# Expert weight forms kept in DRAM by the first token half and read back by the second, in a three-stage float32 kernel

## The chip, the core and the metric

One core of one Trainium2 chip runs the whole program. The metric is the device time of one execution in microseconds; the kernel before has a median of 1330.94 us in three runs (1329.68 to 1335.48).

## What is computed

The reference runs a retention layer, a dense gated layer and a mixture of eight experts with a soft gate on 1536 tokens (2 sequences of 768), model width 512.

```python
state = gamma * state + outer(k[t], v[t]); y[t] = scale * q[t] @ state     # 8 heads of 64
h = x @ w_in; x = (h * clip(h + 3, 0, 6) / 6) @ w_out                      # 2048 hidden
P = exp(x @ w_gate - max)                                                 # then 8 times: rows, columns normalised
for e in range(8):
    out += P[:, e:e + 1] * (relu(x @ w1[e]) @ w2[e])                      # 1024 hidden each
```

## The kernel before

**High and low parts.** Every float32 operand of the dense layer and the experts is split in two: a high part, which ScalarE rounds to TensorE's fast float32 format (`fp32r`), and a low part, the rest, which VectorE gets by subtracting (helper `parts`, lines 499 to 501). A product is three matmuls: high x high, high x low, low x high.

**Stages.** Up to about 60 us: retention. Then the dense layer (lines 348 and 375) to 322.6 us. Then the experts, to the end. Tokens go through the experts in two halves of 768 (`NU` = 2). The 8 experts' 64 hidden tiles of 128 are taken two at a time: 32 pairs per half (`NPR`), 64 in all (`NIT`), each half with the same weights. 

**A pair.** `pair(i)` (line 599) computes the hidden tiles of pair i with a Strassen-like scheme: seven products of sums of weight blocks with sums of token blocks (`product`, line 585, tile `h`, 42 matmuls with 384 columns) in place of eight. ScalarE copies a bank out (line 604, tiles `p`, `u`), VectorE adds another bank to it (line 603), and ScalarE and VectorE make ReLU's high and low parts (`gh`, `gl`, lines 595 and 596). A TensorE product that goes on in a bank waits until the copy of it is out. `outputs(n)` (line 638) multiplies the hidden tiles of two pairs by the second weight (line 660, tile `acc`, 512 columns) and VectorE adds them to `o`, scaled by the gate (line 673). Iteration `it` of the main loop (line 800) weaves pairs 2it and 2it+1 with the outputs of the two pairs before, one chunk of three matmuls at a time, so that 42 + 36 matmuls stand in a pair; the first two pairs have no outputs to weave in.

**Weight forms.** For each pair `w1_forms` (line 503) reads a raw tile of 128 x 2 x 512 (`raw`, DMA of 512 KB, line 494) and makes seven forms of 128 x 256, high and low: four ScalarE and eight VectorE instructions. `w2_parts` (line 528) does the second weight: two and two. Both are generators of `jobs`, one step after each product of the pair: in pair i the first-weight forms of pair i+1, then the second-weight parts of pair i. Each raw tile's successor (two pairs later) is loaded when its forms have read it. The first-weight forms have two buffers, the second-weight parts four. The second half makes the same forms again from the same raw weights.

**The start of the experts.** The forms of pairs 0 and 1 are made while the dense layer ends; the first two raw tiles of the second weight are loaded when the dense layer's memory is free (pool `m2`). In pair 0, the parts of the second weight begin after the fifth product (`slot > 4`).

**The turn.** Before pair 32 the token forms of the second half are made (`x_forms`, nine steps, high and low parts `xh`, `xl`). To cover this, eight chunks of outputs run ahead (`ALONE`), and the rest of `x_forms` and then the forms of pair 33 follow in pair 32. The first half's output tiles (`out`, 256 KB each) are stored in that iteration.

**Order.** The program is issued in the order in which it is written; each engine takes its own instructions in that order. All DMAs here are issued by SP on one queue, and an SP instruction that waits holds back all behind it.

Of the kernel before, what the change touches and what calls it, by code (L numbers as in the profile page):

```python
# [10 lines left out]
F32R = mybir.dt.float32r  # L11
# [9 lines left out]
P = 128  # L21
# [6 lines left out]
BLK = 512  # L28
# [9 lines left out]
NPR = E * F2T // 2  # L38
NIT = NU * NPR
# [17 lines left out]
def kernel(  # L57
# [11 lines left out]
    nc = tc.nc  # L69
    f32 = lambda t: t.bitcast(F32)  # L70
# [6 lines left out]
    def pool(name, side, **kw):  # L77
        open_[name] = c = ExitStack()
        ctx.callback(c.close)
        return c.enter_context(tc.tile_pool(name=name, side=side, **kw))  # L80

    const = pool("const", "left", bufs=1)
    sk = pool("sk", "left", bufs=2)
    xo = pool("xo", "left", bufs=NU)
    xa = pool("xa", "left", bufs=NBLK - 1)
# [20 lines left out]
    raw_t, w_t, pools = {}, {}, {}  # L106
# [379 lines left out]
    B11, T2, T1, T3, B21, B22, T4 = range(7)  # L486
    xf, w1_t, w2_t, raw1, raw2, q_t = {}, {}, {}, {}, {}, {}

    def load_pair(i, part):
        if i >= NIT:  # L490
            return
        f = 2 * (i % NPR)
        t = pools["m2" if part else "m"].tile([P, 2, BLK], F32, tag=f"raw{part}", name=f"raw{part}", bufs=2)
        nc.sync.dma_start(
            out=t, in_=we_in[f:f + 2, :, part * BLK:(part + 1) * BLK].rearrange("t p c -> p t c")
        )
        (raw1, raw2)[part][i] = t

    def parts(hi, lo, t):
        nc.scalar.activation(out=hi, in_=t, func=AF.Copy)  # L500
        nc.vector.tensor_tensor(out=lo, in0=t, in1=f32(hi), op=ALU.subtract)  # L501

    def w1_forms(i):

        r = raw1.pop(i)
        H2 = BLK // 2
        hi = pools["m"].tile([P, 7, H2], F32R, tag="w1hi", name="w1hi", bufs=2)
        lo = pools["m"].tile([P, 7, H2], F32R, tag="w1lo", name="w1lo", bufs=2)
        a11, a12, a21, a22 = (r[:, f, k * H2:(k + 1) * H2] for f in range(2) for k in range(2))
        t = pools["m"].tile([P, 4, H2], F32, tag="s", name="s", bufs=2)  # L510
        parts(hi[:, A11:A12 + 1], lo[:, A11:A12 + 1], r[:, 0].rearrange("p (k c) -> p k c", k=2))
        yield True
        nc.vector.tensor_tensor(out=t[:, S1 - S1], in0=a21, in1=a22, op=ALU.add)
        yield True
        nc.vector.tensor_tensor(out=t[:, S3 - S1], in0=a11, in1=a21, op=ALU.subtract)
        yield True
        nc.vector.tensor_tensor(out=t[:, S2 - S1], in0=t[:, S1 - S1], in1=a11, op=ALU.subtract)
        parts(hi[:, A22], lo[:, A22], a22)
        yield True
        nc.vector.tensor_tensor(out=t[:, S4 - S1], in0=a12, in1=t[:, S2 - S1], op=ALU.subtract)  # L520
        load_pair(i + 2, 0)
        yield True
        for n in range(2):
            parts(hi[:, S1 + 2 * n:S3 + 1 + 2 * n], lo[:, S1 + 2 * n:S3 + 1 + 2 * n], t[:, 2 * n:2 * n + 2])
            yield True
        w1_t[i] = (hi, lo)

    def w2_parts(i):
        r = raw2.pop(i)
        hi = pools["m2"].tile([P, 2, BLK], F32R, tag="w2hi", name="w2hi", bufs=4)  # L530
        lo = pools["m2"].tile([P, 2, BLK], F32R, tag="w2lo", name="w2lo", bufs=4)
        for f in range(2):
            parts(hi[:, f], lo[:, f], r[:, f])
            yield True
        load_pair(i + 2, 1)
        w2_t[i] = (hi, lo)

    def x_forms(u):

        b11, b21, b12, b22 = (  # L540
            y2[u][:, 2 * k:2 * k + 2, j * SB:(j + 1) * SB] for j in range(2) for k in range(2)
        )
        xf.clear()

        def form(n, t):
            xf[n] = tuple(pools["xf"].tile([P, 2, SB], F32R, tag=f"x{n}{p}", name=f"x{p}") for p in "hl")
            parts(*xf[n], t)

        def tmp():
            t = pools["m"].tile([P, 4, BLK // 2], F32, tag="s", name="s", bufs=2)  # L550
            return t.rearrange("p a b -> p (a b)")[:, 0:2 * SB].rearrange("p (k c) -> p k c", k=2)

        form(B11, b11)
        yield True
        form(B21, b21)
        yield True
        t1 = tmp()
        nc.vector.tensor_tensor(out=t1, in0=b12, in1=b11, op=ALU.subtract)
        t2 = tmp()
        nc.vector.tensor_tensor(out=t2, in0=b22, in1=t1, op=ALU.subtract)  # L560
        yield True
        form(T2, t2)
        yield True
        form(T1, t1)
        yield True
        t4 = tmp()
        nc.vector.tensor_tensor(out=t4, in0=b21, in1=t2, op=ALU.subtract)
        t3 = tmp()
        nc.vector.tensor_tensor(out=t3, in0=b22, in1=b12, op=ALU.subtract)
        yield True  # L570
        form(T3, t3)
        yield True
        form(B22, b22)
        yield True
        form(T4, t4)
        yield True
# [22 lines left out]
    def pair(i):  # L599

        tmp = lambda n: pools["m2"].tile([P, SB], F32, tag=n, name=n, bufs=2)
        bank = lambda n: ps_s.tile([P, BLK], F32, tag=n, name="h")
        add = lambda out, a, b: nc.vector.tensor_tensor(out=out, in0=a, in1=b, op=ALU.add)  # L603
        copy = lambda out, a: nc.scalar.activation(out=out, in_=a, func=AF.Copy)  # L604

        bx = bank("s0")
        product(i, bx, A11, B11, True, True)
        p1 = tmp("p1")
        copy(p1, bx[:, 0:SB])
        yield  # L610
        by = bank("s1")
        product(i, by, A12, B21, True, True)
        yield
        add(p1, by[:, 0:SB], p1)
        product(i, bx, S2, T2, False, True)
        u2 = tmp("u2")
        copy(u2, bx[:, 0:SB])
        yield
        relu_parts(i, 0, 0, p1)
        bz = bank("r")  # L620
        product(i, bz, S1, T1, True, True)
        p5 = tmp("p5")
        copy(p5, bz[:, 0:SB])
        yield
        product(i, bx, S3, T3, False, True)
        add(p5, bx[:, 0:SB], p5)
        yield
        product(i, bz, S4, B22, False, True)
        relu_parts(i, 1, 1, p5)
        yield  # L630
        add(u2, bz[:, 0:SB], u2)
        product(i, bx, A22, T4, False, True)
        yield
        relu_parts(i, 0, 1, u2)
        relu_parts(i, 1, 0, bx[:, 0:SB])
        yield
# [44 lines left out]
    def drain(it):  # L681
        for _ in it:
            pass
# [7 lines left out]
    with tc.manual_schedule():  # L691
# [59 lines left out]
        forming = None  # L751
# [3 lines left out]
        for s in range(NSF):  # L755
            if s == NSF - NBLK * GROUPS[-1]:
                open_["wx"].close()
            if s == LASTB:
# [5 lines left out]
                forming = itertools.chain(x_forms(0), w1_forms(0), w1_forms(1))  # L764
# [35 lines left out]
        for it in range(NIT // 2 + 1):  # L800
            outs = outputs(it - 1) if it else iter(())
            chunks = 4 * TU if it else 0
            jobs = []
            for i in (2 * it, 2 * it + 1):
                if i < NIT:

                    ahead = i % NPR and i + 1 < NIT
                    jobs.append([w1_forms(i + 1)] if ahead else [])
                    jobs[-1].append(w2_parts(i))
            alone = 0  # L810
            if it and (2 * it) % NPR == 0 and 2 * it < NIT:

                forming = itertools.chain(x_forms(2 * it // NPR), w1_forms(2 * it + 1))
                alone = ALONE
                for n in range(alone):
                    next(outs)
                    if n % 2 == 0:
                        next(forming)
                jobs[0].insert(0, forming)
            done = slot = 0  # L820
            for n, i in enumerate(range(2 * it, min(2 * it + 2, NIT))):
                job = itertools.chain(*jobs[n])
                for _ in pair(i):
                    slot += 1
                    while done * 16 < (chunks - alone) * slot:
                        next(outs)
                        done += 1
                    if it or slot > 4:

                        for _ in range(1 if not it or (alone and slot < 6) else 2):  # L830
                            next(job, None)
                    if it and slot % 2 == 0:
                        next(gate, lambda: None)()
                drain(job)
            drain(outs)
            for i in (2 * it - 2, 2 * it - 1):
                w2_t.pop(i, None)
# [65 lines left out]
```

## Time and profile before

| | |
|---|---|
| median of three runs | 1330.94 us |
| the profiled execution, first to last instruction | 1329.5 us |
| TensorE busy | 1318.1 us, 99% |
| VectorE busy | 897.7 us, 68% |
| ScalarE busy | 567.6 us, 43% |
| DMA, mean | 76 GB/s |
| DMA on SP's queue | 99.71 MB, 22.2% of 16 engines' span |

The profile gives no other time of its own execution than the span, 1329.5 us; the fastest run is 0.2 us above it. Matmuls are pipelined: one shows as 0.39 us, but they start 0.23 us apart, so starts and groups are read, not single durations. "Share" of the DMA is the mean busy share of 16 DMA engines in a stretch.

### The profile page before, as it was taken

What the parts mean: (1) busy time and instruction counts of PE and PEld (TensorE: products, weight loads), DVE (VectorE), ACT (ScalarE), POOL (GpSimd) and SP (SyncE); (2) the same over time, 40 slices, a digit from 0 to 9 for tenths busy, and PEclk for the clock granted to TensorE, in tenths of its full rate; (3) what the DMA queues carried; (4) which work ended last, traced back from release to release, by engine and by line L of the source; (5) the groups of instructions that cost most, each with busy time, mean ns of one, the idle gap of its engine ahead of it and who ended that gap; (6) DMA issues with size and microseconds to landing.
All of it is one profiled execution on the core that took longest, in us unless ns stands there. A gap on an engine that the chain in (4) does not pass through costs nothing.

```text
span 1329.5 us, 17332 instructions
## 1 busy us (share of the span) xinstructions
PE 1318.1 (99%) x6776; PEld 1164.4 (88%) x6776; DVE 897.7 (68%) x1704; ACT 567.6 (43%) x1072; POOL 26.7 (2%) x30
## 2 busy tenths in 40 slices
PE   8999999999999999999999999999999999999998
PEld 7888888888888999999999998899999999999997
DVE  6877657338688666666666668766666666666663
ACT  5567445224534343434443344444343434443340
POOL 4300000000000000000000000000000000000000
PEclk9999999999999999999999999999999999999999
DMA  8633222002212122111221211312222111221201
GB/s 309 217 95 96 64 64 80 0 0 66 93 49 75 68 67 76 64 64 64 67 77 65 78 64 57 119 64 76 68 67 77 64 64 64 71 73 65 79 17 48
DMA packets 44990, 100.82 MB, mean 76 GB/s; under 512 B 3430, under 2 KB 3430, under 8 KB 44908
## 3 DMA queue, kind: packets, MB, share of 16 engines
q1 hardware_dynamic: 44908, 99.71, 22.2%
q8 instruction: 53, 0.87, 0.3%
q14 instruction: 29, 0.24, 0.1%
HBM read 96.55 MB, written 3.15 MB: 75 GB/s over the span
## 4 chain that ended last, share of the span: by engine, by line
PE 90%; DVE 3%; ACT 1%; DMA 0%; issue 0%; ACTq 0%
PE acc L660 38%; PE h L585 33%; PE acc L375 10%; PE h L348 9%; DMA raw<-in_we 0%; DVE gl L596 0%; DVE xl L501 0%; DVE w1lo L501 0%; DVE o L673 0%; DVE w2lo L501 0%; PE l L405 0%; DVE o L669 0%; DVE p L603 0%; ACT w2hi L500 0%; ACT xh L500 0%
## 5 line engine op out<-in xcount | busy, mean ns | idle before, releaser
L585 PE MATMUL h<-xh,w1hi 128*128 128x384 f32 x896 | 301.8, 337 | 0.9 <-ACT p L604 0.9
L660 PE MATMUL acc<-w2hi,gl 128*128 128x512 f32 x768 | 301.7, 393 | 0.0
L585 PE MATMUL h<-xh,w1lo 128*128 128x384 f32 x896 | 301.1, 336 | 0.0
L585 PE MATMUL h<-xl,w1hi 128*128 128x384 f32 x896 | 300.8, 336 | 0.2 <-DVE xl L501 0.2
L660 PE MATMUL acc<-w2hi,gh 128*128 128x512 f32 x768 | 299.6, 390 | 0.0
L660 PE MATMUL acc<-w2lo,gh 128*128 128x512 f32 x768 | 298.8, 389 | 0.0
L673 DVE SCALAR_TENSOR_TENSOR o<-acc,pm,o 128x512 f32<-128x512 f32 x174 | 130.7, 751 | 143.7 <-PE acc L660 143.7
L585 PEld LDWEIGHTS h<-xl,w1hi 128*128 128x128 f32 x896 | 168.2, 188 | 20.3 <-DVE xl L501 0.9
L585 PEld LDWEIGHTS h<-xh,w1hi 128*128 128x128 f32 x896 | 168.3, 188 | 19.8 <-ACT p L604 1.6
L660 PEld LDWEIGHTS acc<-w2hi,gl 128*128 128x128 f32 x768 | 144.1, 188 | 30.9
L585 PEld LDWEIGHTS h<-xh,w1lo 128*128 128x128 f32 x896 | 168.2, 188 | 0.0
L660 PEld LDWEIGHTS acc<-w2lo,gh 128*128 128x128 f32 x768 | 144.3, 188 | 13.0
L660 PEld LDWEIGHTS acc<-w2hi,gh 128*128 128x128 f32 x768 | 143.8, 187 | 13.0
L604 ACT ACTIVATE p<-h 128x384 f32<-128x384 f32 x128 | 62.9, 491 | 203.2 <-PE h L585 203.1
L501 DVE TENSOR_TENSOR w1lo<-raw,w1hi 128x512 fp32r<-128x512 f32 (+1 forms) x128 | 71.1, 555 | 77.4 <-ACT w1hi L500 77.3
L501 DVE TENSOR_TENSOR w1lo<-s,w1hi 128x512 fp32r<-128x512 f32 x128 | 87.9, 688 | 37.9 <-ACT w1hi L500 37.7
L604 ACT ACTIVATE u<-h 128x384 f32<-128x384 f32 x64 | 31.5, 492 | 173.5 <-PE h L585 173.5
L595 ACT ACTIVATE gh<-p 128x384 fp32r<-128x384 f32 x128 | 66.7, 521 | 57.5 <-DVE p L603 57.5
L501 DVE TENSOR_TENSOR w2lo<-raw,w2hi 128x512 fp32r<-128x512 f32 x128 | 87.2, 683 | 4.7 <-ACT w2hi L500 4.7
L595 ACT ACTIVATE gh<-u 128x384 fp32r<-128x384 f32 x64 | 33.6, 525 | 127.3 <-DVE u L603 127.3
L500 ACT ACTIVATE w1hi<-s 128x512 fp32r<-128x512 f32 x128 | 79.7, 624 | 3.3 <-DVE s L520 1.9
L348 PE MATMUL h<-xhi,wlo 128*128 128x512 f32 x192 | 74.9, 390 | 0.5 <-DVE wlo L136 0.5
(107 smaller groups left out, 1681.3 us busy)
## 6 DMA issues: line engine op xcount, KB each, us to landing
raw<-in_we SPq DMA_DIRECT2D x128, 512.0 KB, 3.4
raw<-in_wf SPq DMA_DIRECT2D x32, 512.0 KB, 3.7
qk<-in_qk SPq DMA_DIRECT2D x12, 512.0 KB, 6.9
kv<-in_kv SPq DMA_DIRECT2D x12, 512.0 KB, 6.0
out<-o SPq DMA_DIRECT2D x12, 256.0 KB, 2.0
tab<-in_tab SPq DMA_DIRECT2D x1, 40.5 KB
gk<-in_gk SPq DMA_DIRECT2D x1, 24.0 KB, 3.5
wg_raw<-in_wg SPq DMA_DIRECT2D x1, 16.0 KB, 7.7
```

Source lines behind the costliest of these rows:

```text
L348: nc.tensor.matmul(h, w[:, ks], x[:, k], start=(n == 0), stop=(n == 3 * KT - 1))
L375: nc.tensor.matmul(acc_b[i], l, r, start=(f == 0 and j == 0), stop=(f == nf - 1 and j == 2))
L500: nc.scalar.activation(out=hi, in_=t, func=AF.Copy)
L501: nc.vector.tensor_tensor(out=lo, in0=t, in1=f32(hi), op=ALU.subtract)
L585: nc.tensor.matmul(bank[:, 0:SB], l[:, w, ks], r[:, k], start=(start and n == 0), stop=(stop and n == 5), skip_group_check=True,)
L595: nc.scalar.activation(out=hi, in_=t, func=AF.Relu)
L604: copy = lambda out, a: nc.scalar.activation(out=out, in_=a, func=AF.Copy)
L660: nc.tensor.matmul(acc, l[:, cs], r[:, f % 2], start=(f == 0 and k == 0), stop=(f == 3 and k == 2))
L673: nc.vector.scalar_tensor_tensor(out=o[:, tt], in0=acc, scalar=sc, in1=o[:, tt], op0=ALU.mult, op1=ALU.add)
```

## The change

In the first half (`i < NPR`) each finished form tile is stored to a tile in DRAM (`keep`, right after the forms are made). In the second half no raw weights are loaded and no forms are made: `fetch` loads the form tile from DRAM in one DMA at the place where the forms' generator would have run. For that, high and low parts share one tile (`w1`: 128 x 2 x 7 x 256, `w2`: 128 x 2 x 2 x 512), with the same number of buffers as before.

```diff
+    dr = ctx.enter_context(tc.tile_pool(name="dr", bufs=1, space=bass.MemoryType.DRAM))
...
+    kept = {}
+
+    def keep(part, i, t):
+
+        kept[part, i] = d = dr.tile(list(t.shape), F32R, tag=f"kept{part}_{i}", name=f"kept{part}")
+        nc.sync.dma_start(out=f32(d), in_=f32(t))
+
+    def fetch(part, i):
+        if part:
+            t = pools["m2"].tile([P, 2, 2, BLK], F32R, tag="w2", name="w2", bufs=4)
+        else:
+            t = pools["m"].tile([P, 2, 7, BLK // 2], F32R, tag="w1", name="w1", bufs=2)
+        nc.sync.dma_start(out=f32(t), in_=f32(kept[part, i - NPR]))
+        (w1_t, w2_t)[part][i] = (t[:, 0], t[:, 1])
+        yield True
+
     def load_pair(i, part):
-        if i >= NIT:
+        if i >= NPR:
             return
-        f = 2 * (i % NPR)
+        f = 2 * i
...
-        hi = pools["m"].tile([P, 7, H2], F32R, tag="w1hi", name="w1hi", bufs=2)
-        lo = pools["m"].tile([P, 7, H2], F32R, tag="w1lo", name="w1lo", bufs=2)
+        w = pools["m"].tile([P, 2, 7, H2], F32R, tag="w1", name="w1", bufs=2)
+        hi, lo = w[:, 0], w[:, 1]
...
         w1_t[i] = (hi, lo)
+        keep(0, i, w)
...
-        hi = pools["m2"].tile([P, 2, BLK], F32R, tag="w2hi", name="w2hi", bufs=4)
-        lo = pools["m2"].tile([P, 2, BLK], F32R, tag="w2lo", name="w2lo", bufs=4)
+        w = pools["m2"].tile([P, 2, 2, BLK], F32R, tag="w2", name="w2", bufs=4)
+        hi, lo = w[:, 0], w[:, 1]
...
         w2_t[i] = (hi, lo)
+        keep(1, i, w)
...
-                    jobs.append([w1_forms(i + 1)] if ahead else [])
-                    jobs[-1].append(w2_parts(i))
+                    make = w1_forms if i + 1 < NPR else lambda n: fetch(0, n)
+                    jobs.append([make(i + 1)] if ahead else [])
+                    jobs[-1].append(w2_parts(i) if i < NPR else fetch(1, i))
...
-                forming = itertools.chain(x_forms(2 * it // NPR), w1_forms(2 * it + 1))
+                forming = itertools.chain(x_forms(2 * it // NPR), fetch(0, 2 * it + 1))
```

On VectorE the program loses 320 instructions, on ScalarE 192; on SP 64 loads of 512 KB go, 64 stores and 64 loads of form tiles come. TensorE's instructions stay the same.

SP at the end of the dense layer, before: raw tiles of the first weight for pairs 0 to 3 (four rows), of the second weight for pairs 0 and 1 (two rows), then on.

```order
L494 DMA raw_2480<-in_we 128x2x512
L494 DMA raw_2482<-in_we 128x2x512
L494 DMA raw_2650<-in_we 128x2x512
L494 DMA raw_2716<-in_we 128x2x512
L494 DMA raw_2746<-in_we 128x2x512
L494 DMA raw_2748<-in_we 128x2x512
L494 DMA raw_2818<-in_we 128x2x512
```

The same place in the changed kernel (line 511 is the raw load, line 495 the store; `w_2602` and `w_2696` are the first-weight forms of pairs 0 and 1, `w_2799` the second-weight parts of pair 0).

```order
L511 DMA raw_2482<-in_we 128x2x512
L511 DMA raw_2484<-in_we 128x2x512
L511 DMA raw_2651<-in_we 128x2x512
L495 DMA kept_2694<-w_2602 128x3584
L511 DMA raw_2718<-in_we 128x2x512
L495 DMA kept_2724<-w_2696 128x3584
L511 DMA raw_2750<-in_we 128x2x512
L511 DMA raw_2752<-in_we 128x2x512
L511 DMA raw_2821<-in_we 128x2x512
L495 DMA kept_2823<-w_2799 128x2048
```

Two stores of 128 x 3584 now stand ahead of the second weight's first raw load (`raw_2750`, before `raw_2746`).

SP at the turn, before: the raw loads go on, and the output stores of the first half stand among them.

```order
L494 DMA raw_7088<-in_we 128x2x512
L494 DMA raw_7130<-in_we 128x2x512
L678 DMA out<-o 128x512 x4
L494 DMA raw_7348<-in_we 128x2x512
L494 DMA raw_7360<-in_we 128x2x512
L494 DMA raw_7408<-in_we 128x2x512
L678 DMA out<-o 128x512
```

The same place in the changed kernel (line 502 is the load of a kept tile, line 697 the output; `w_7109`, `w_7357` and `w_7397` are the first-weight forms of pairs 32, 33 and 34, `w_7359` the second-weight parts of pair 32).

```order
L495 DMA kept_7052<-w_7033 128x2048
L502 DMA w_7109<-kept_2694 128x3584
L495 DMA kept_7126<-w_7111 128x2048
L697 DMA out<-o 128x512 x3
L502 DMA w_7357<-kept_2724 128x3584
L502 DMA w_7359<-kept_2823 128x2048
L697 DMA out<-o 128x512
L502 DMA w_7397<-kept_2919 128x3584
```

The forms of pair 33 are now a load on SP that stands behind three output stores; it is the first row on SP that pair 33's products need.

## Rows read from the trace of the kernel before

**Rows 1.** The page: busy us, share of the span, instructions of each engine.
```profile
PE 1318.1 (99%) x6776; PEld 1164.4 (88%) x6776; DVE 897.7 (68%) x1704; ACT 567.6 (43%) x1072; POOL 26.7 (2%) x30
```
**Rows 2.** Windows: stretch, length, busy us (instructions) per engine, PEclk, DMA share, GB/s.
```profile
800.00:900.00 100.00, 99.32 (x497) 89.02 (x496) 75.76 (x139) 46.38 (x92) 0.00 (x0) 1.00 0.25 84
900.00:1000.00 100.00, 100.00 (x504) 90.52 (x503) 67.43 (x129) 39.21 (x82) 0.00 (x0) 1.00 0.21 69
...
1307.00:1325.00 18.00, 18.00 (x82) 14.96 (x81) 5.54 (x8) 0.49 (x1) 0.00 (x0) 1.00 0.18 66
```
**Rows 3.** The chain that ended last: start us, us, what (expert stage's start, and end).
```profile
322.77 5.46 DMA raw<-in_we
...
328.25 0.64 ACT w2hi L500
...
328.92 0.69 DVE w2lo L501
...
332.09 0.39 ACT p L604
...
332.52 6.70 PE h L585 x36
339.22 1.37 PE acc L660 x6
...
1307.38 18.38 PE acc L660 x81
```
**Rows 4.** Timelines of VectorE, SP and TensorE at the turn: start us, us, engine, line.
```profile
823.93 0.74 DVE L673 SCALAR_TENSOR_TENSOR o<-acc,pm,o 128x512 f32<-128x512 f32 x1
...
824.70 7.01 SPq L678 DMA_DIRECT2D out<-o  x2
...
829.68 0.34 PE L585 MATMUL h<-xh,w1hi 128*128 128x384 f32 x1
...
833.82 0.44 PE L585 MATMUL h<-xh,w1hi 128*128 128x384 f32 x1 [0.52 <-ACT p L604]
```
**Rows 5.** The page's costliest groups, one of the forms' instructions: busy us, mean ns.
```profile
L501 DVE TENSOR_TENSOR w1lo<-s,w1hi 128x512 fp32r<-128x512 f32 x128 | 87.9, 688 | 37.9 <-ACT w1hi L500 37.7
```
**Rows 6.** Timeline of SP's DMA issues near the program's start, first and last of six.
```profile
2.05 0.43 SPq L226 DMA_DIRECT2D qk<-in_qk  x1
...
4.67 0.50 SPq L259 DMA_DIRECT2D kv<-in_kv  x1
```
**Rows 7.** The DMA view, issues at 2.05 and at 4.67 us: KB, us to landing.
```profile
qk<-in_qk SPq DMA_DIRECT2D x1, 512.0 KB, 5.1
...
kv<-in_kv SPq DMA_DIRECT2D x1, 512.0 KB, 9.7
```
**Rows 8.** Windows as in rows 2: fast loads, raw expert loads alone, output stores.
```profile
15.00:20.00 5.00, 4.89 (x56) 4.29 (x54) 3.32 (x6) 3.18 (x5) 1.96 (x3) 1.00 1.05 409
...
325.50:326.80 1.30, 1.30 (x10) 1.30 (x9) 0.01 (x1) 0.88 (x2) 0.00 (x0) 1.00 0.98 288
...
1315.00:1320.00 5.00, 5.00 (x24) 4.14 (x23) 1.40 (x2) 0.00 (x0) 0.00 (x0) 1.00 0.28 105
```
**Rows 9.** Timeline of SP at the end of the dense layer: raw loads.
```profile
320.97 0.37 SPq L494 DMA_DIRECT2D raw<-in_we  x1
...
322.77 0.37 SPq L494 DMA_DIRECT2D raw<-in_we  x1
```
**Rows 10.** The DMA view: issues at 320.97 and 322.77 us, and the last outputs.
```profile
raw<-in_we SPq DMA_DIRECT2D x1, 512.0 KB, 3.4
...
raw<-in_we SPq DMA_DIRECT2D x1, 512.0 KB, 5.5
...
out<-o SPq DMA_DIRECT2D x6, 256.0 KB, 2.0
```
**Rows 11.** Timeline of VectorE: the ends of the first two pairs' forms.
```profile
317.33 1.29 DVE L501 TENSOR_TENSOR w1lo<-s,w1hi 128x512 fp32r<-128x512 f32 x2
...
320.82 1.48 DVE L501 TENSOR_TENSOR w1lo<-s,w1hi 128x512 fp32r<-128x512 f32 x2
```

## The prediction

> **What bounds the kernel now.** I read the busy shares first, then the busy time by stretches, then the chain of waits, then the timelines at the places where the chain leaves TensorE, and last the DMA queue. The reader is to see that TensorE is busy 1318.1 of 1329.5 us [rows 1] and that a stretch in the middle of the second token half has no idle time at all: 100.00 us of 100 with 504 matmuls [rows 2]. A pair of f-tiles is 42 matmuls of `h` and 36 of `acc`, so 78 / 504 x 100 = 15.5 us. VectorE (67 us of 100) and ScalarE (39) are below it there; their work is cover, not path. Does TensorE's pace hang on them all the same? In the last 18 us VectorE has 5.5 us of work and ScalarE 0.5 [rows 2], and 81 matmuls of `acc` take 18.38 us, 0.227 us each; at 339 us, with both engines at work, six take 1.37 us, 0.228 each [rows 3]. So it does not. The clock is granted in full in all these stretches.
>
> So the work that the change removes is not on the path, and only the places where TensorE waits can move. Two matter. At 332.1 us the chain goes from a weight load that landed late through ScalarE and VectorE to TensorE's next product [rows 3]. At 833 us TensorE waits 0.52 us for ScalarE's `p` [rows 4]; the whole stretch 800 to 900 us has 0.68 us of idle TensorE [rows 2].
>
> **What is removed.** In the second half 32 pairs lose 10 VectorE and 6 ScalarE instructions each: 320 and 192. The costliest of VectorE's is 688 ns [rows 5], so at most 320 x 0.69 = 220 us of VectorE go. On the path this is worth the idle time that it causes, 0.52 us at 833 us, where ScalarE is behind because of forms of pair 33 and VectorE likewise: with the step before the matmul I count 0.6 us. The other waits lie ahead of the second half. Gain: 0.6 us. The 64 raw loads of the second half go too; none was waited for.
>
> **What is added.** Per pair a store of 128 x 3584 x 4 B = 1.835 MB (first weight) and one of 128 x 2048 x 4 B = 1.049 MB (second weight) in the first half, and the same two as loads in the second: 64 stores, which come back as 64 loads. Rates come from loads: five loads of 0.524 MB that queue behind one issued at 2.05 us land between 2.05 + 5.1 = 7.15 and 4.67 + 9.7 = 14.37 us [rows 6, 7], that is 5 x 0.524 / 7.22 = 363 GB/s, and one after another. The fastest stretch had 409 GB/s, the one with 2 KB rows of `in_we` 288 at a share of 0.98 [rows 8]. For stores I have only the output: 105 GB/s at a DMA share of 0.28 is 375 GB/s for a full share [rows 8]. So a first-weight transfer takes 4.9 us as a store, 5.05 as a load; 4.5 at 409 and 6.4 at 288 are the ends.
>
> Steady state, first half: 2.88 MB at 375 is 7.7 us, two raw loads at 288 are 3.6 us, together 11.3 of the 15.5 us of a pair. That fits. Who waits: raw loads are issued a pair and more before use, and a form's buffer is written again two pairs after its store was issued. Cost 0, with the DMA's spare 4.2 us per pair as cover; what it costs without that is a rival below. Steady state, second half: SP issues the load for the next pair when TensorE has finished the pair before, a whole pair (15.5 us) ahead of need, against some 7 us. Cost 0.
>
> **The start of the expert stage.** Here the order listing decides. The second-weight raw load of pair 0 used to go out at 322.77 us, 1.8 us behind a first-weight raw load [rows 9], and landed 5.5 us later [rows 10]. Now two stores of 1.835 MB stand ahead of it on the same queue: one that SP can issue when VectorE ends the first forms, 317.33 + 1.29 = 318.6 us, one when it ends the second, 320.82 + 1.48 = 322.3 us [rows 11]. A load alone lands 3.4 us after issue [rows 10], of which 0.524 MB at 288 GB/s is 1.8; 1.6 is start and completion. From the first store on, the queue does not run dry: 318.6 + 1.6 + 4.9 (store) + 1.8 (raw) + 4.9 (store) + 1.8 (the load in question) = 333.6 us, against 328.23 by the chain. ScalarE reads this load in program order, and behind it stand the copy and the ReLUs that free TensorE's banks; from landing to TensorE's next product the chain takes 4.3 us [rows 3], and TensorE was already waiting 0.4 us there, so no slack absorbs it: **+5.4 us**. With transfers of 4.5 us it is +4.6, with 6.4 it is +8.4.
>
> **The turn to the second half.** The first-weight load for pair 33 stands on SP behind three output stores. The third waits for VectorE's `o` at 823.93 us and went out at 824.70 [rows 4]; the load follows about 0.4 us later, at 825.1. Its engine time begins when that output's 0.262 MB are through: 825.7 + 0.7 = 826.4; + 5.05 + 0.6 = 832.05 us. TensorE wants pair 33 at 829.68 us [rows 4]: a stall of 2.4 us, which takes the place of the 0.6 us. Net **+1.8 us**; ends: 831.5 us and +1.2, 833.4 us and +3.1. The forms that used to be made there needed no such transfer, because the raw data had long landed.
>
> **Sum:** 5.4 + 1.8 = 7.2 us; ends 5.8 and 11.5. Against the profiled execution 1329.5 + 7.2 = 1336.7. The median of the runs lies 1.4 us above that execution, so the forecast is 1330.9 + 7.2 = 1338.1, say 1338.0 us. A measurement can tell about 0.5% of this kernel, 6.65 us, from no change, so the forecast lies just above that limit (1337.6).
>
> What no row shows is a load queued behind a store. The loads at the start landed one after another [rows 6, 7], which is why I take it as in order. The Trainium skill, DMA: Bandwidth & Descriptors, section Queues, rings and completion order, says that each DMA engine takes its descriptors in ring order and that the semaphore's update lands only after every earlier write of that engine; by that rule the load cannot be reported ahead of the stores, and the sum stands; without it rival B is open. The same page, in the section on the anatomy of one DMA, says the receipt of a write is heaviest when the target is HBM. The trace does not bear that out: an output of 256 KB lands 2.0 us after issue [rows 10], less than a load. By the page the start would cost perhaps 0.5 to 1 us more (estimate from that page's fixed 2 us), 1338.8 us; I keep the rows.
>
> **The rivals.**
> - B, not slower: the load of pair 0 is served beside the stores instead of behind them. For it: reading and writing sides may overlap, and no row shows the mix. Against: the landings one by one [rows 6, 7]. If it shares the engines with the second store, 0.524 MB need 2 x 1.8 us from about 326, so it lands at about 330: +1.8 at the start, or nothing if served first. With +1.2 to 1.8 at the turn: 1332 to 1334.5 us. It decides when the load lands before 330.
> - C, much slower: the DMA engines cannot take the first half. Two raw loads leave 15.5 - 3.6 = 11.9 us for 2.88 MB; under 242 GB/s every pair gets longer. At 200 GB/s it is 14.4 + 3.6 = 18.0, 2.5 us x 30 pairs = 75 us, 1413 us; barely below the limit, or with VectorE slowed by the traffic, some 10 us more than forecast. Against: 375 GB/s for the outputs [rows 8].
> - D, faster: TensorE gains pace where the other two engines fall idle, 1% of half the expert stage, 5 us, and the stalls come out small: some 1324 us. Against: the equal pace in rows 3.
>
> **Chances.** Forecast 0.65, B 0.20, C 0.10, D 0.05. Of the forecast's own span (5.8 to 11.5 us) about three fifths lies beyond 6.65 us: slower 0.40 + 0.10 = 0.50, same 0.25 + 0.20 = 0.45, faster 0.05. The range takes in B and the ends: 1332 to 1345.
>
> **What would show it.** Right: TensorE idle about 5 to 6 us around 332 us with the raw load at the head of the chain, landing at 333 to 334; about 2.4 us before pair 33's first product, ended by the load; no other new idle time; VectorE below 40 us per 100 in the second half; DMA share about 0.7 in the first. Wrong: the first raw load landing by 330 us, idle TensorE in every pair of the first half, or more than 504 matmuls per 100 us in the second.

## The result

The changed kernel takes 1343.41 us (median of 4 runs, 1341.63 to 1345.87) against 1333.14 us of the kernel before in the same session (4 runs, 1329.68 to 1335.48): a ratio of 1.0081, 95% interval 1.0061 to 1.01. It is slower by some 10 us. The forecast was slower by 7.2 us, to 1338.0 us, with a range of 1332 to 1345 us.

The page of the changed kernel: busy us, share of the span, instructions of each engine, to be held against [rows 1].

```profile
PE 1323.3 (99%) x6776; PEld 1169.9 (87%) x6776; DVE 750.0 (56%) x1384; ACT 476.4 (35%) x880; POOL 27.2 (2%) x30
```

VectorE lost 148 us of work and ScalarE 91, TensorE none, and the span grew from 1329.5 to 1342.2 us. The work that went was cover. The windows (columns as in [rows 2]) tell where the time went.

```profile
300.00:400.00 100.00, 95.27 (x482) 82.82 (x481) 72.25 (x163) 47.12 (x94) 0.00 (x0) 0.97 0.61 230
...
500.00:600.00 100.00, 100.00 (x504) 90.59 (x503) 68.17 (x131) 41.10 (x85) 0.00 (x0) 1.00 0.70 259
...
800.00:900.00 100.00, 96.01 (x473) 86.09 (x472) 47.26 (x75) 27.11 (x52) 0.00 (x0) 0.98 0.55 209
900.00:1000.00 100.00, 100.00 (x504) 90.47 (x503) 37.62 (x64) 21.80 (x45) 0.00 (x0) 1.00 0.50 192
```

In the middle of either half TensorE has no idle time and starts 504 matmuls per 100 us, as before, at 259 and at 192 GB/s. Of the stretches from 300 us on, the two with the start of the experts and with the turn lose most, and in both the granted clock is below 1.00. TensorE's waits in the changed kernel (engine, line, waited for: us in total, times, longest):

```profile
PE h L604 <- ACT p L623: 4.5, 1, 4.5
PE h L604 <- DMA w<-kept: 3.8, 1, 3.8
...
PE gc L459 <- DVE pm L453: 0.9, 2, 0.7
```

Two long ones, at the two places that the prediction named. The last row is a product of the gate, near 411 us; before the change it waits a little less:

```profile
PE gc L458 <- DVE pm L452: 0.6, 2, 0.4
```

The chain of waits at each of them (start us, us, what):

```profile
324.25 9.65 DMA raw<-in_we
...
333.92 0.64 ACT w L517
...
338.18 8.72 PE h L604 x36
...
832.71 0.33 SPq L697
...
833.14 8.47 DMA w<-kept
...
841.66 2.29 PE h L604 x6
...
846.82 1.04 PE h L604 x6
```

At the start the raw load of pair 0's second weight takes 9.65 us instead of 5.46 [rows 3]. At the turn the load of pair 33's forms is issued when the third output store is out and takes 8.47 us. In both places the matmuls after the wait are slow: 36 of them take 8.72 us, 6.70 before [rows 3]; six take 2.29 us, and 1.04 a little later. The windows show why, in the column before the DMA's (granted clock; 0.50 of 2.4 GHz is 1.2 GHz):

```profile
334.00:336.00 2.00, 0.00 (x0) 0.00 (x0) 1.42 (x3) 1.48 (x3) 0.00 (x0) 1.00 0.28 104
336.00:338.00 2.00, 0.00 (x0) 0.00 (x0) 1.41 (x4) 1.15 (x3) 0.00 (x0) 0.55 0.20 37
338.00:340.00 2.00, 1.82 (x6) 1.82 (x7) 1.75 (x4) 0.65 (x2) 0.00 (x0) 0.50 1.00 312
340.00:342.00 2.00, 2.00 (x8) 2.00 (x7) 1.06 (x4) 0.90 (x2) 0.00 (x0) 0.50 0.98 417
342.00:344.00 2.00, 2.00 (x11) 2.00 (x10) 0.95 (x4) 0.80 (x2) 0.00 (x0) 0.75 0.06 25
...
840.00:842.00 2.00, 0.34 (x1) 0.34 (x2) 0.00 (x0) 0.00 (x0) 0.00 (x0) 0.84 0.98 392
842.00:844.00 2.00, 2.00 (x7) 2.00 (x7) 0.00 (x0) 0.00 (x0) 0.00 (x0) 0.50 1.10 454
```

TensorE stands still at both places, the granted clock falls to 0.50 while it does, and the matmuls after the wait run at about half speed until it is back. At the start it falls with the DMA at 37 GB/s, at the turn with 392.

The DMA view of the changed kernel: the issues at 320.13, 322.45 and 323.81 us (two stores and the raw load between them), then the page's medians (KB each, us to landing):

```profile
kept<-w SPq DMA_DIRECT2D x1, 1792.0 KB, 6.6
...
raw<-in_we SPq DMA_DIRECT2D x1, 512.0 KB, 5.7
...
kept<-w SPq DMA_DIRECT2D x1, 1792.0 KB, 8.9
```
```profile
kept<-w SPq DMA_DIRECT2D x32, 1792.0 KB, 6.4
w<-kept SPq DMA_DIRECT2D x32, 1792.0 KB, 7.3
```

The transfers land in the order of their issue (326.8, 328.1, 332.7 us); the raw load and the second store land later after issue than such transfers do in the median or alone (3.4 us for a raw load in [rows 10]).

To see what each piece costs, I took the starts of the first matmuls of pairs 0, 2, 32, 33 and 34 and of the last matmul from TensorE's timeline in each kernel. The table gives the time between them (us; e1 to e6 are the experiments below):

| piece | before | changed | e1 | e2 | e3 | e4 | e5 | e6 |
|---|---|---|---|---|---|---|---|---|
| pairs 0 and 1 | 15.44 | 21.64 | 16.57 | 21.86 | 16.49 | 21.47 | 21.53 | 16.24 |
| pairs 2 to 31 | 478.16 | 478.48 | 478.47 | 478.44 | 478.47 | 478.44 | 478.48 | 478.48 |
| pair 32, with the wait behind it | 13.51 | 17.48 | 17.10 | 13.51 | 13.51 | 13.51 | 17.67 | 13.51 |
| pair 33 | 13.59 | 14.35 | 14.49 | 12.81 | 12.81 | 13.59 | 12.81 | 12.81 |
| pair 34 to the end of TensorE | 482.08 | 482.09 | 482.08 | 482.08 | 482.08 | 482.08 | 482.08 | 482.08 |

For the changed kernel: +6.20 + 0.32 + 3.97 + 0.76 + 0.01 = +11.3 us. The other 1.5 us of the two profiles' difference lie ahead of the first expert product (322.57 against 324.06 us), where the change does nothing; over these profiles that product starts anywhere between 320.8 and 326.2 us. All of that spread lies in the retention: from the first product of the dense layer to the first of the experts every profile takes 265.1 to 265.2 us, and the dense layer starts at 55.6 to 61.0 us. In e5's profile, the latest, TensorE is busy as long in the first 10 us as before the change but gets through fewer matmuls (before, then e5):

```profile
0.00:10.00 10.00, 8.48 (x65) 6.73 (x67) 4.48 (x10) 3.85 (x7) 2.81 (x8) 1.00 0.76 268
0.00:10.00 10.00, 8.48 (x39) 6.10 (x39) 3.06 (x8) 2.48 (x4) 2.38 (x7) 1.00 0.79 270
```

Its `sc` matmuls, issued two by two, start 0.21 us apart until 17.3 us and 0.11 after; before the change they are 0.11 apart from 6.5 us on. The clock column does not show this. In the changed kernel's profile the granted clock is 0.94 and 0.89 in 10 to 20 and 20 to 30 us, after a wait of 1.9 us for `qk`, and 1.00 before the change. The pieces above are free of all this, the medians are not.

### The profile page after: what moved, and what is told of

It reads as the page before. It is cut to its first block, busy times and chain, and to the rows that moved or that the text cites. A ratio compares the mean times of both kernels' runs of the same rounds, so it can differ in the third digit from the quotient of the medians.

```text
span 1342.2 us, 16919 instructions
## 1 busy us (share of the span) xinstructions
PE 1323.3 (99%) x6776; PEld 1169.9 (87%) x6776; DVE 750.0 (56%) x1384; ACT 476.4 (35%) x880; POOL 27.2 (2%) x30
## 4 chain that ended last, share of the span: by engine, by line
PE 90%; DVE 3%; DMA 1%; ACT 0%; issue 0%; SPq 0%
PE acc L679 38%; PE h L604 33%; PE acc L376 10%; PE h L349 9%; DMA raw<-in_we 1%; DMA w<-kept 1%; DVE w L518 0%; PE l L406 0%; DVE gl L615 0%; DVE o L692 0%; DVE xl L518 0%; DVE o L688 0%; ACT xh L517 0%; DVE pm L470 0%; DVE r L450 0%
## 5 line engine op out<-in xcount | busy, mean ns | idle before, releaser
L604 PE MATMUL h<-xh,w 128*128 128x384 f32 x1792 | 531.6, 338 | 8.4 <-ACT p L623 4.5
L679 PE MATMUL acc<-w,gh 128*128 128x512 f32 x1536 | 474.3, 390 | 0.0
L604 PEld LDWEIGHTS h<-xh,w 128*128 128x128 f32 x1792 | 332.6, 189 | 27.0 <-ACT p L623 4.9
L679 PEld LDWEIGHTS acc<-w,gh 128*128 128x128 f32 x1536 | 282.7, 188 | 26.0
L604 PE MATMUL h<-xl,w 128*128 128x384 f32 x896 | 302.4, 338 | 0.2 <-DVE xl L518 0.2
L679 PE MATMUL acc<-w,gl 128*128 128x512 f32 x768 | 302.2, 393 | 0.0
L604 PEld LDWEIGHTS h<-xl,w 128*128 128x128 f32 x896 | 169.3, 189 | 20.2 <-DVE xl L518 0.9
L679 PEld LDWEIGHTS acc<-w,gl 128*128 128x128 f32 x768 | 144.4, 188 | 30.8
L518 DVE TENSOR_TENSOR w<-raw,w 128x512 fp32r<-128x512 f32 (+1 forms) x128 | 79.1, 619 | 45.9 <-ACT w L517 45.6
L349 PE MATMUL h<-xhi,whi 128*128 128x512 f32 x192 | 75.4, 393 | 0.0
```

The source lines that it names most:

```text
L349: nc.tensor.matmul(h, w[:, ks], x[:, k], start=(n == 0), stop=(n == 3 * KT - 1))
L604: nc.tensor.matmul(bank[:, 0:SB], l[:, w, ks], r[:, k], start=(start and n == 0), stop=(stop and n == 5), skip_group_check=True,)
L679: nc.tensor.matmul(acc, l[:, cs], r[:, f % 2], start=(f == 0 and k == 0), stop=(f == 3 and k == 2))
```

## The experiments

My theory was that the loss is two waits, each with a stretch of half clock behind it, and nothing else. Each time is set against the kernel before in the same session, 1330.86 us for e1 to e4 and 1330.81 for e5 to e8. The rivals were that the traffic costs something in every pair, and that the half clock comes from the traffic and not from TensorE's rest.

**e1: the second store moved behind the raw loads (start).**

```diff
-        keep(0, i, w)
+        if i == 1:
+            late.append((0, i, w))
+        else:
+            keep(0, i, w)
...
         for i in range(2):
             load_pair(i, 1)
+        for a in late:
+            keep(*a)
```

> The store of pair 1's first-weight forms goes to SP behind the first two raw loads of the second weight, so one store instead of two stands ahead of pair 0's raw load; all else as in the changed kernel. Theory (the loss is two waits, each followed by a stretch of TensorE at half clock): the wait of 4.5 us in the first pairs shrinks to the 0.4 us of before or under 1 us, no stretch at a granted clock of 0.5 follows it, and the time falls by 4.1 + 2.0 = some 6 us, to 1.0034 to 1.0040 of before. Rival (the half clock and most of the loss come from the traffic, not from the wait): the wait goes, TensorE still falls to 0.5, and the time falls by 4 us at most.

Measured: 1337.44 us against 1330.86, 6.6 us over before where the changed kernel is 10.3 over in its session; ratio 1.006 (1.0038 to 1.0081), an interval that is too wide to tell 4 us of gain from 6. The profile tells more. Chain, waits and a window of e1:

```profile
322.25 6.61 DMA raw<-in_we
...
333.14 6.69 PE h L607 x36
```
```profile
PE h L607 <- DMA w<-kept: 3.4, 1, 3.4
...
PE h L607 <- ACT p L626: 1.5, 1, 1.5
```
```profile
334.00:338.00 4.00, 4.00 (x24) 3.79 (x23) 3.50 (x9) 2.24 (x6) 0.00 (x0) 1.00 0.91 355
```

The wait at the start fell from 4.5 to 1.5 us, not to under 1: the load still lands 6.6 us after issue with one store ahead of it. The 36 matmuls take 6.69 us, as before; after a wait of 1.5 us the clock is at 1.00, though the DMA moves 355 GB/s. The piece "pairs 0 and 1" fell by 5.1 us, and the kernel's pieces together are 5.9 us over before, 5.4 less than the changed kernel's. The medians alone fall by 3.7 us and would leave the rival standing; the clock and the pieces put it out.

**e2: the load of pair 33 ahead of the output stores (turn).**

```diff
-                forming = itertools.chain(x_forms(2 * it // NPR), fetch(0, 2 * it + 1))
+                drain(fetch(0, 2 * it + 1))
+                forming = x_forms(2 * it // NPR)
```

> The load of pair 33's first-weight forms is issued ahead of the output stores of the turn, some 16 us earlier; all else as in the changed kernel. Theory: the wait of 3.8 us at the turn and the 1.7 us of half clock behind it go, the 0.5 us wait of before does not come back; the time falls by 5 to 5.5 us, to 1.0040 of before. Rival (the load only moves the queue on, and the next loads, of pairs 32 and 34, are late in its place): the wait shows at another product of pairs 33 or 34, and the time falls by under 2 us.

Measured: 1336.71 us, 5.9 us over before, ratio 1.0049 (1.0031 to 1.0067). TensorE's longest waits:

```profile
PE h L604 <- ACT p L623: 4.4, 1, 4.4
PE warm L732 <- DVE rs L721: 1.5, 1, 1.5
```

The first is the one at the start, the second lies at the kernel's beginning. The wait for the load is gone, no other has come at the turn, and pair 33 takes 12.81 us, 0.78 less than before the change. The two pieces give -3.97 - 1.54 = -5.5 us against the changed kernel, as the theory expected.

**e3: both.**

> Both moves together. Theory: nothing of the loss is left, and the wait of 0.5 us at the turn of before is gone: 0.998 to 1.001 of before, DMA traffic as in the changed kernel. Rival (part of the loss is spread over all pairs, as slower steps under 200 to 260 GB/s): 1.002 to 1.004 of before, with fewer than 504 matmuls per 100 us in the middle of a half. Second rival (VectorE and ScalarE at rest let TensorE go faster): under 0.997, over 504 matmuls per 100 us in the second half.

Measured: 1332.03 us (12 runs) against 1330.86, ratio 1.0004, interval 0.999 to 1.0018: the loss is gone, and there is no gain. The table leaves +1.05 at the start, +0.31 in pairs 2 to 31, -0.78 at the turn: +0.6 us. Its windows:

```profile
500.00:600.00 100.00, 100.00 (x504) 90.53 (x503) 66.70 (x128) 40.07 (x84) 0.00 (x0) 1.00 0.67 252
900.00:1000.00 100.00, 100.00 (x504) 90.54 (x503) 38.87 (x66) 22.11 (x45) 0.00 (x0) 1.00 0.48 184
```

504 matmuls per 100 us at 252 GB/s of stores and loads, and 504 with VectorE at 39 us of 100 instead of 67. Neither the spread-out cost nor the faster TensorE is there.

**e4: the stores alone.** The first half stores as in the changed kernel; the second half loads raw weights and forms them again.

```diff
-        keep(0, i, w)
+        if i < NPR:
+            keep(0, i, w)
...
-                forming = itertools.chain(x_forms(2 * it // NPR), fetch(0, 2 * it + 1))
+                forming = itertools.chain(x_forms(2 * it // NPR), w1_forms(2 * it + 1))
```

> The stores of the first half stay, but the second half loads raw weights and makes the forms again, as before: the stores alone. Theory: only the start is lost, 4.1 us of wait and 2.0 us of half clock, +6 us, 1.0045 of before, and the turn shows its old waits of 0.5 us. Rival (the reading back is all of it, the stores are free): 1.000 to 1.001.

Measured: 1339.35 us, ratio 1.0059 (1.004 to 1.0077). Its longest wait (two in all, the other 0.5 us as at the turn before the change):

```profile
PE h L606 <- ACT p L625: 5.0, 2, 4.5
```

By the table the start costs 6.03 us, pairs 2 to 31 0.28, and the turn and the second half nothing, +6.3 us in all, 1.0047, within the interval. The stores are not free, and what they cost is the start alone.

**e5: TensorE kept busy through the wait at the turn.**

```diff
+FILL = 24
...
+                if i == NPR + 1:
+                    t = ps_s.tile([P, BLK], F32, tag="s1", name="idle")
+                    for _ in range(FILL):
+                        nc.tensor.matmul(t[:, 0:SB], w1_t[i - 1][0][:, 0, 0:P], xf[B11][0][:, 0], start=True, stop=True)
```

> The changed kernel with 24 matmuls of 128x384 (some 4 us, into a bank that nothing reads) ahead of pair 33's first product, where TensorE waits 3.8 us for the load. Theory (the half clock comes from TensorE's own idle time): the wait is filled, the load lands when it did, the granted clock stays at 1.0 there, pair 33's first six matmuls take 1.04 to 1.1 us instead of 2.29; the time falls by 1.5 to 2 us against the changed kernel. Rival (the half clock comes from the DMA traffic or from the load's landing): the granted clock falls to 0.5 all the same and the time does not fall.

Measured: 1340.89 us, ratio 1.0071 (1.0054 to 1.0088). The chain, and the window of the two microseconds before pair 33:

```profile
839.87 4.16 PE idle L847 x24
844.03 1.04 PE h L605 x6
```
```profile
842.00:844.00 2.00, 2.00 (x13) 2.00 (x12) 0.00 (x0) 0.00 (x0) 0.00 (x0) 1.00 0.98 397
```

TensorE reaches pair 33 no sooner (17.67 us against 17.48), but the clock stays at 1.00 with the DMA as busy as before, and pair 33 takes 12.81 us instead of 14.35. The load lands 8.2 us after issue, at 843.4 us, before the filling ends. So the half clock comes from TensorE's rest, and it cost 1.54 us there. The ratio is 0.001 lower than that of the changed kernel, 1.3 us, but the two intervals overlap; the verdict rests on the profile.

**e6: no store ahead of the first raw load.** From e3, both late stores follow a raw load each.

```diff
-        if i == 1:
+        if i < 2:
             late.append((0, i, w))
...
         for i in range(2):
             load_pair(i, 1)
-        for a in late:
-            keep(*a)
+            keep(*late[i])
```

> As with both moves, but the first-weight store of pair 0 too goes behind the second weight's raw load of pair 0, and that of pair 1 behind the raw load of pair 1: no store stands ahead of pair 0's load. Theory (the 1.4 us left at the start are the one store still ahead of it): the load lands 1 us earlier after its issue (5.5 instead of 6.5 us), the wait for ScalarE's copy falls to 0.4 to 0.6 us, the time by under 1 us: 0.998 to 1.001 of before. Rival: the store now ends late for the next forms, ScalarE waits for it in pair 1, and as much is lost there.

Measured: 1332.16 us, ratio 1.0016 (1.0003 to 1.003), a little above the expected 0.998 to 1.001. Its wait at the start:

```profile
PE h L607 <- ACT p L626: 0.9, 1, 0.9
```

The load lands 6.0 us after issue, and the piece "pairs 0 and 1" is 0.25 us shorter than in e3. That is half of what was expected, too little for the median to show; the chain there now runs through the store of pair 0's forms, as the rival said, though ScalarE rests only 0.16 us there. No gain beyond e3 is seen from this order.

**e7 and e8: more traffic.** From e3, with the second-weight stores made twice (e7), and with all stores from pair 2 on made twice (e8).

```diff
+        if part == 1:
+            d2 = dr.tile(list(t.shape), F32R, tag=f"twin{part}_{i}", name=f"twin{part}")
+            nc.sync.dma_start(out=f32(d2), in_=f32(t))
```

In e8 the condition is `i > 1` in place of `part == 1`.

> As with both moves, and every second-weight store of the first half is made twice (1.05 MB more per pair, to another place in DRAM). Theory (the traffic is hidden as long as it fits in a pair's 15.5 us): a pair's transfers take 4.6 + 2 x 2.65 + 3.1 = 13 us, so nothing is lost: 0.999 to 1.003 of before, DMA share near 0.85, 504 matmuls per 100 us. Rival (every MB costs, through slower steps of the engines or late raw loads): 1.004 or more.

> As with both moves, and all stores of the first half from pair 2 on are made twice. Theory: a pair's transfers take 2 x (4.6 + 2.65) + 2.6 to 3.6 = 17.1 to 18.1 us, over its 15.5; the queue falls behind and each pair lasts as long as its transfers: 1.6 to 2.6 us x 30 pairs, 48 to 78 us, 1380 to 1410 us, DMA share near 1.0 in the first half, the second half as before. Rival (the stores' time is only the landing, the engines have far more room): under 1345 us.

Measured: e7 1331.47 us, ratio 1.0006 (0.9992 to 1.0019); e8 1357.93 us (two runs), ratio 1.0203 (1.0182 to 1.0224). A window of e7, then two of e8, the landing of e8's first-weight stores between 400 and 800 us, and e8's longest wait of TensorE:

```profile
500.00:600.00 100.00, 100.00 (x504) 90.52 (x503) 66.21 (x128) 39.64 (x83) 0.00 (x0) 1.00 0.85 326
```
```profile
400.00:500.00 100.00, 99.56 (x499) 89.64 (x499) 72.28 (x149) 40.69 (x84) 0.00 (x0) 1.00 1.01 412
500.00:600.00 100.00, 96.81 (x479) 85.23 (x478) 61.50 (x122) 38.72 (x78) 0.00 (x0) 1.00 1.02 419
```
```profile
kept<-w SPq DMA_DIRECT2D x25, 1792.0 KB, 21.5
```
```profile
PE h L610 <- DMA w<-kept: 8.7, 1, 8.7
```

At 326 GB/s nothing is lost: e7's pieces are those of e3 within 0.2 us. At 419 GB/s and a full share it is: a store that landed 6.4 us after issue in the changed kernel now lands after 21.5 us (medians), and 479 matmuls are started per 100 us, 16.3 us per pair instead of 15.5 (a pair's 6.82 MB at 419 GB/s are 16.3 us). The mechanism is the expected one, the size is not: 27 us instead of 48 to 78, since the engines move 419 GB/s, not the 1.835 MB in 4.6 us (399 GB/s) that I had put in, and the queue needs until about 500 us to fall behind. The backlog also delays a load of kept forms at the turn: 8.7 of the 27 us are one wait of TensorE for it, the first load of the second half.

**e9: the load behind the late load moved away.**

```diff
-                    jobs[-1].append(w2_parts(i) if i < NPR else fetch(1, i))
+                    if i == NPR + 1:
+                        jobs[-1].append(fetch(1, i - 1))
+                    if i != NPR:
+                        jobs[-1].append(w2_parts(i) if i < NPR else fetch(1, i))
```

> The changed kernel with the second-weight load of pair 32, which follows 0.4 us behind the first-weight load of pair 33 on SP, moved into the next pair's jobs, so that the latter has only the output store ahead of it and nothing behind it. In the changed kernel it lands 8.5 us after its issue, against 7.0 forecast. If the load behind it takes engine time from it (the sixteen engines drift apart and start on the next transfer): it lands 7.6 to 7.9 us after issue, and TensorE's wait falls from 3.8 to about 3 us. If a transfer of 1.835 MB behind an output simply takes that long: 8.3 us or more, and a wait of 3.7 us or more. In both cases the granted clock falls to 0.5 after the wait.

Measured: 1345.06 us against 1332.04, one run each. Its chain:

```profile
833.32 8.23 DMA w<-kept
...
841.60 2.29 PE h L604 x6
```

8.2 us instead of 8.5, between the two numbers and nearer the second; TensorE waits 3.6 us for it. The load behind costs little. But that such a load behind an output store takes over 8 us does not follow. In e3 the same load, with nothing ahead, lands 7.1 us after issue, and so does the next one of its size there (issued at 831.18 us), which stands 0.4 us behind an output store and has a load behind it. In the changed kernel the load at 857.43 us, in the same order, lands after 7.2. The DMA view tells the two kinds apart. It has this row from the issue of the late load to its landing, in the changed kernel (833 to 841.6 us), in e1 and in e9:

```profile
q8 instruction: 1, 0.02, 0.7%
```

The same view has no such row for the two loads that land after 7.1 and 7.2 us (e3, 831 to 838.3 us; changed kernel, 857 to 864.6 us):

```profile
w<-kept SPq DMA_DIRECT2D x1, 1792.0 KB, 7.1
...
w<-kept SPq DMA_DIRECT2D x1, 1792.0 KB, 7.2
```

The row is one transfer of 16 KB that the profile calls `instruction`; in the changed kernel it runs on the DMA engines at 838.7 us, 5.5 us after the load's issue. In that profile 23 loads of this size find the queue empty but for at most an output store: the four with such a transfer 4 to 6 us after their issue land after 8.0 to 8.8 us, the other 19 after 7.1 to 7.7. So the extra microsecond goes with that transfer. No run here moves the transfer, so that it is the cause is likely, not shown.

## Why the prediction was right, and where its sizes were off

- **What bounds the kernel, and that the removed work is worth only its waits:** right. 320 VectorE and 192 ScalarE instructions went, and pair 34 to the end takes 482.08 us with them (before, e4) and without (e2, e3). So rival D is out. The 0.6 us at the turn are 0.78 (e2, e3: 13.59 to 12.81).
- **Steady state at no cost in both halves:** right, by e3 and the table. The 0.3 us in pairs 2 to 31 are the gate's wait (`gc`), 0.9 us instead of 0.6; why that grew was not tried (with e8's heavier traffic it is 0.6). The cover holds at 326 GB/s (e7) and is gone at 419 (e8). Rival C is out.
- **The start, a load held behind two stores:** the place and the mechanism are right: two stores ahead 9.65 us to landing, one 6.6 (e1), none 6.0 (e6). The landings are in the order of issue, and rival B is out. The size was 4.2 us of landing (9.65 - 5.46), not 5.4. From the first store's issue (320.13 us) to the load's landing (333.90) the four transfers took 13.8 us, where the sum has 15.0. By their landings the first store took 6.63 us (1.6 + 4.9 in the sum), the raw load behind it 1.34 (1.8), the second store 4.64 (4.9; 396 GB/s, not 375), the load in question 1.16 (1.8). So the two terms "1.8", read from a stretch at 288 GB/s, account for 1.1 of the 1.2 us. That the load landed near the forecast's 333.6 us is chance: in this profile the experts start 1.5 us later.
- **The turn:** the issue time was right within 0.1 us (833.14, less the 8.0 us that pair 32 starts later, is 825.1, as forecast). The wait was 3.97 us instead of 2.4, because the load landed 8.5 us after issue, not 7.0. The term "5.05 + 0.6" behind an output is about 0.2 us short of what such loads take in e3 and later in the changed kernel (7.1 and 7.2 us); the rest goes with the instruction transfer beside the load (e9), which no row of the prediction shows.
- **What was missing:** the half clock after a wait. The terms +5.4 and +1.8 counted the wait alone. It cost 2.0 us at the start (8.72 - 6.70) and 1.5 us at the turn (e5), 3.5 of the 11.3 us. With it the forecast would have been 10.7 us, beside the 10.3 measured. The kernel before has no such wait in this stage, its longest is 0.5 us, so its rows did not price it, but a wait of 5 us was in the forecast and its price should have been asked for. The Trainium skill, TensorE: Matmul & The Clock Gate, section Loop structure matters more than you think, gives a loop that waits for a DMA ahead of its matmuls as its bad example: TensorE idles and drops to half its clock. These traces agree: 0.50 after waits of 4.5 and 3.8 us, 1.00 after 1.5 us (e1).

Too large at the start, too small at the turn, one cost left out: 7.2 us forecast, 11.3 by the profiles, 10.3 by the medians. That the result lies in the range is in part luck: the two sizes err in opposite directions, and the upper end was priced from first-weight transfers at 288 GB/s, where the second store at the start moved at 396; the half clock filled that room. A load reported late because of write receipts in DRAM was not seen: the output stores of the changed kernel land 2.0 to 2.2 us after issue at the turn and at the end, as in [rows 10]. The section on the anatomy of one DMA, from which the prediction took the Trainium skill's fixed 2 us, is about DMAs that GpSimd issues; here SP issues them all.

## What to carry to other kernels

When an engine that is not the bound gets less work, ask only which waits of the bounding engine that ends; here it was 0.8 us of 1330. Price added DMAs by what stands behind them in the issuing queue at the places where the cover is thin (a stage's first loads, a change of phase) and not by the mean share: moving one store behind two loads and one load ahead of three stores took the whole loss back at the same traffic. Price a new wait of TensorE of several microseconds with the half-clock stretch behind it.

## What was not expected of the hardware

- After rests of 4.5 and 3.8 us TensorE's granted clock is at 0.50 for the first microseconds of work (at the start it is back between 342 and 344 us), whether the DMA moved 37 or 392 GB/s when it fell; matmuls into an unread bank in the wait at the turn keep it at 1.00 (e5). In the changed kernel's profile it also falls for a while after a wait of 1.9 us in the retention.
- Stores with rows of 14 and 8 KB and raw loads among them run at 419 GB/s with a full queue (e8), more than the fastest stretch before, 409 [rows 8]. TensorE loses nothing beside 326 GB/s (e7), and a VectorE instruction takes 0.52 us on average there as before.
- Loads of 1.835 MB land 7.1 to 7.7 us after issue, and 8.0 to 8.8 where an instruction transfer falls into their second half (changed kernel, 19 and 4 loads). One of these four fell on the one load that TensorE was waiting for.
- The part ahead of the experts, which no kernel here changes, takes 320.8 to 326.2 us from profile to profile, and the difference arises in the first 60 us. It is as large as the spread between runs of one kernel (1329.68 to 1335.48 us before the change). That it is the same thing is likely, not shown.
